# Attention by two pairs of heads in quarters of the TensorE array, beside a bilinear feed-forward network

## The chip, the cores and the metric

One core of a Trainium2 chip. The metric is the device time of one launch in microseconds (us); lower is better.

TensorE is called PE here, ScalarE ACT, VectorE DVE, GpSimd POOL; "PEld" in a profile is PE's loading of weights. "FFN" is the feed-forward network.

## The reference, cut to what matters

```python
batch, n_heads, seq, head_dim = (8, 12, 448, 64)          # q, k, v float32
n_tokens, d_model, d_ff = (3584, 768, 1536)               # w_a, w_b, w_out float64

q_n, k_n = rmsnorm(q, g_q), rmsnorm(k, g_k)               # over head_dim
scores = q_n @ k_n.T / sqrt(64)
attn = softmax(scores)
x = (attn @ v) as (8 * 448, 12 * 64)
out = ((x @ w_a) * (x @ w_b)) @ w_out
```

## The kernel before

A small planner inside the kernel (`Plan`) takes every operation with an estimated time, an engine, a priority and the tiles it needs. It plays the run through and then emits the instructions in the order it found. The order on each engine is therefore fixed when the kernel is built.

There are eight batches of twelve heads. Two batches make a block. Attention of a block has to be complete before its FFN (Strassen-like, seven products for eight) can start; the FFN of one block and the attention of the next are put between each other. At the start there is no FFN to put anywhere, and DVE has 18 weight factors to round there and in the first FFN.

Attention in the kernel before takes a pair of heads at a time, with 112 of the 448 keys as one piece:

```python
def scores(p, c, chain):                       # piece c of 4, two heads on two halves of the rows
    t = scs[p, c] = ps_s.tile([SP, 2, 512], FP32, tag="sc", name="sc")       # SP = 112
    for e in range(2):
        rows = slice(e * D, (e + 1) * D)                                     # D = 64
        nc.tensor.matmul(t[:, e, 0:S], lhsT=qkTs[p][rows, 1, c * SP:(c + 1) * SP],
                         rhs=qkTs[p][rows, 0, :], start=True, stop=True)
    # ... then ACT: E = exp(scale of the key * score)

def values(p, c, chain):                       # two heads on two halves of the columns
    for e in range(2):
        nc.tensor.matmul(os_[p][e * D:(e + 1) * D, :], lhsT=xs["v", p][:, e, c * D:(c + 1) * D],
                         rhs=ETs[p, c][:, e], start=(c == 0), stop=(c == NJ - 1))

def sums_over_keys(p, cs, chain):              # same form as values
    parts = [ETs[p, c] for c in cs] if p < WIDE else [sums[p]]     # first 12 pairs: all on PE
    for n, x in enumerate(parts):
        for e in range(2):
            nc.tensor.matmul(sus[p][e * D:(e + 1) * D, :], lhsT=ones, rhs=x[:, e], ...)
    # ... then: ACT copies the sums to a tile "rec" (3 buffers); one row per head goes by DMA
    # onto many partitions, DVE takes reciprocals there, and two DMAs bring them back into "rec"
```

A fp32 matmul is two passes of the array in the trace. Three forms of the array are in use: full (128 rows, 128 columns: FFN and transposes), rows (two heads on 64 rows each: scores), columns (two heads on 64 columns each: values and sums).

Of the kernel before, what the change touches and what calls it, by code (L numbers as in the profile page):

```python
# [25 lines left out]
class Plan:  # L26
# [11 lines left out]
    RATE, LANDING = 300.0, 2.5  # L38
# [32 lines left out]
    def run(self):  # L71
# [40 lines left out]
        while any(cands.values()):  # L112
            best = None
            for e, cs in cands.items():
                f = free.get(e, 0.0) if e else 0.0
                at = {}
                for n in cs:
                    t = buffers(n)
                    if t is not None:
                        t = t[0]  # L120
                        turn = self.TURN if ops[n][5] != modes.get(e) else 0.0
                        at[n] = max(f, ready[n], t, port if ops[n][10] else 0.0,
                                    sent[ops[n][11] - 1 - self.LANES] if ops[n][11] else 0.0) + turn
                if at:
                    t = min(at.values()) + (0.2 if e == "PE" else 0.05)
                    n = min((n for n in at if at[n] <= t), key=lambda n: (ops[n][2], n))
                    if best is None or at[n] < best[0]:
                        best = at[n], e, n
# [38 lines left out]
def kernel(  # L167
# [53 lines left out]
    ones = const.tile([SP, D], FP32, name="ones")  # L221
    gain = const.tile([P, 1], FP32, name="gain")
    expo = const.tile([SP, 2 * 2 * NJ], FP32, name="expo")
# [25 lines left out]
    ROUND, FACTOR, SQUARE, ADD_UP, TIMES = "DVE", "DVE", "ACT", "POOL", "POOL"  # L249
# [45 lines left out]
    def fast_body(ld, wk, ps_s, ps_o, ps_mm, dram):  # L295
        plan = Plan()
        op, tile_of = plan.op, plan.tile
        NORM = 4.0
        FEW = S // 8
        WARM = 4  # L300
        APART = 4
        LEAD = 12
        WIDE = 12
# [38 lines left out]
        def factors(n, key, early, after):  # L342

            last = n >= len(order)
            st = tile_of(f"st{n}", "st", 3)

            def begin():
                sts[n] = ld.tile([P, 7, KH * P], FP32, tag="st", name="st", bufs=3)
# [10 lines left out]
            for part in range(2):  # L359
# [9 lines left out]
                op("ACT", 0.45, key - 1.5, load, after, [f"{row}/{part}"], kb=768)  # L369
# [21 lines left out]
        def stream(beta, n, f=None):  # L391

            st = tile_of(f"st{beta}.{n}", "st", 3)

            def load():
                t = sts[beta, n] = ld.tile([P, 7, KH * P], FP32, tag="st", name="st", bufs=3)
# [5 lines left out]
            op("SP", 0.5, 12.0 * beta + n / 2, load, reads, [f"{st}/{x}" for x in range(7)] + ["streaming"], new=[st],  # L402
# [3 lines left out]
        xs, rs, qns, qkTs, pts, scs, ETs, sums, sus, os_, quads, hTs = ({} for _ in range(12))  # L406

        def loads(p, nm):
            b, h0 = p // HP, 2 * (p % HP)
            src = {"q": q, "k": k, "v": v}[nm]  # L410
            t = tile_of(f"{nm}{p}", nm, 2)

            def emit():
                if nm == "k":
                    x = ld.tile([SP, NJ, 2, D], FP32, tag=nm, name=nm + "_sb")
                    nc.sync.dma_start(x, src[b, h0:h0 + 2].rearrange("h (p j) d -> p j h d", j=NJ))
                else:
                    x = ld.tile([SP, 2, NJ * D], FP32, tag=nm, name=nm + "_sb")
                    nc.sync.dma_start(x, src[b, h0:h0 + 2].rearrange("h (p j) d -> p h (j d)", j=NJ))
                xs[nm, p] = x  # L420
            op("SP", 0.5 if nm != "k" else 0.9, p - (2.3 if nm == "v" else 2.5), emit, [], [t], new=[t], kb=230 if nm != "k" else 400)

        def normalize(p):
# [4 lines left out]
            def begin():  # L428
                rs[p] = wk.tile([SP, 2, 2 * NJ], FP32, tag="ms", name="ms", bufs=3)
            op(None, 0.0, key, begin, [], [f"{ms}/q", f"{ms}/k"], new=[ms])  # L430

            def sums(s, nm):
                sq = tile_of(f"sq{nm}{p}", "sq", 1)

                def square():
                    x = xs[nm, p]
                    t = xs["sq", nm, p] = wk.tile([SP, 2 * NJ, D], FP32, tag="sq", name="sq")
# [3 lines left out]
                op("ACT", 0.65, key, square, [f"{nm}{p}"], [sq], new=[sq])  # L441
                op("DVE", 0.69, key, lambda: nc.vector.tensor_reduce(rs[p][:, s], xs["sq", nm, p], AX, ALU.add), [sq], [f"{ms}/{nm}"])  # L442

            def roots(a, b, names):
                msf = lambda: rs[p][:, a:b].rearrange("p s n -> p (s n)")
                op("DVE", 0.18, key, lambda: nc.vector.tensor_scalar(msf(), msf(), 1.0 / D, 1e-6, ALU.mult, ALU.add), [], names)  # L446
                op("POOL", 1.7 if b - a == 1 else 2.95, key,
                   lambda: nc.gpsimd.tensor_tensor(msf(), msf(), expo[:, 0:2 * NJ * (b - a)], ALU.pow), [], names)  # L448

            def apply():  # L450
                qns[p] = wk.tile([SP, NJ, 2, D], FP32, tag="qn", name="qn")
# [3 lines left out]
                    rs[p][:, 0].rearrange("p (h j) -> p h j ()", j=NJ).to_broadcast([SP, 2, NJ, D]),  # L455
                    ALU.mult)
            sums(0, "q")
            if p < APART:
                roots(0, 1, [f"{ms}/q"])
            sums(1, "k")  # L460
# [5 lines left out]
            op("DVE", 0.7, key, apply, [f"{ms}/q", f"q{p}"], [qn], new=[qn], lock=True)  # L466

        def transposes(p):
            qkT = tile_of(f"qkT{p}", "qkT", 2)
            key = p - 0.5 if p < LEAD else p - 1.5  # L470
            for n, nm in ((1, "k"), (0, "q")):

                pt = f"pt{nm}{p}" if p < LEAD else f"pt{p}"
                own = n == 1 or p < LEAD
                if own:
                    tile_of(pt, *(("mm", 2) if p < LEAD else ("sc", 2)))

                def turn(n=n, nm=nm):
                    if p < LEAD:
                        t = pts[p, n] = ps_mm.tile([P, 512], FP32, tag="mm", name="pt")  # L480
                    else:
                        if n == 1:
                            pts[p] = ps_s.tile([P, 2, 512], FP32, tag="sc", name="pt")
                        t = pts[p, n] = pts[p][:, n]
                    x = xs["k", p] if n == 1 else qns[p]
                    for j in range(NJ):
                        nc.tensor.transpose(t[:, j * SP:(j + 1) * SP], x[:, j].rearrange("p h d -> p (h d)"), ident[0:SP, 0:SP])  # L487

                def take(n=n):
                    if n == 1:  # L490
                        qkTs[p] = wk.tile([P, 2, S], FP32, tag="qkT", name="qkT", bufs=2)
                        nc.scalar.copy(qkTs[p][:, 1], pts[p, 1][:, 0:S])
                    else:
                        nc.scalar.activation(qkTs[p][:, 0], pts[p, 0][:, 0:S], AF.Copy, scale=gain[:, 0:1])  # L494
                after = [] if p < LEAD else [f"half{p - 1}"]
                op("PE", 0.45, key, turn, [f"{nm}{p}" if n else f"qn{p}"] + after, [f"{pt}/{n}"], new=[pt] if own else [],
                   mode="full", chain=f"T{p}")
                op("ACT", 0.55 if n else 0.68, key, take, [f"{pt}/{n}", "gain"], [f"{qkT}/{n}"], new=[qkT] if n else [])

        def scores(p, c, chain):  # L500
            sc, E = tile_of(f"sc{p}.{c}", "sc", 2), tile_of(f"E{p}.{c}", "ET", 4)

            def product():
                t = scs[p, c] = ps_s.tile([SP, 2, 512], FP32, tag="sc", name="sc")
                for e in range(2):
                    rows = slice(e * D, (e + 1) * D)
                    nc.tensor.matmul(t[:, e, 0:S], lhsT=qkTs[p][rows, 1, c * SP:(c + 1) * SP],  # L507
                                     rhs=qkTs[p][rows, 0, :], start=True, stop=True)

            def exps():  # L510
                E = ETs[p, c] = wk.tile([SP, 2, S], FP32, tag="ET", name="ET", bufs=4)
                for e in range(2):
                    nc.scalar.activation(E[:, e], scs[p, c][:, e, 0:S], AF.Exp,  # L513
                                         scale=rs[p][:, 1, 2 * c + e:2 * c + e + 1])
            op("PE", 0.76, p, product, [f"qkT{p}/0", f"qkT{p}/1"], [sc] + ([f"scored{p}"] if c == NJ - 1 else [f"half{p}"] if c == 1 else []), new=[sc],
               mode="rows", chain=chain)
            op("ACT", 1.12, p, exps, [sc, f"ms{p}/k"], [E], new=[E])

        def values(p, c, chain):
            o = f"o{p}"  # L520
            if c == 0:
                tile_of(o, "o", 1)

            def product():
                if c == 0:
                    os_[p] = ps_o.tile([P, S], FP32, tag="o", name="o")
                for e in range(2):
                    nc.tensor.matmul(os_[p][e * D:(e + 1) * D, :], lhsT=xs["v", p][:, e, c * D:(c + 1) * D],  # L528
                                     rhs=ETs[p, c][:, e], start=(c == 0), stop=(c == NJ - 1))
            op("PE", 0.76, p, product, [f"E{p}.{c}", f"v{p}"], [o], new=[o] if c == 0 else [], mode="cols", chain=chain)  # L530

        def add_up(p, c):

            t = f"sum{p}"
            if c == 1:
                tile_of(t, "sum", 1)

            def emit():
                if c == 1:
                    sums[p] = wk.tile([P, 2, S], FP32, tag="sum", name="sum")[0:SP]  # L540
                    nc.vector.tensor_tensor(sums[p], ETs[p, 0], ETs[p, 1], ALU.add)  # L541
                else:
                    two[ADD_UP].tensor_tensor(sums[p], sums[p], ETs[p, c], ALU.add)  # L543
            if c == 1:
                op("DVE", 1.12, p, emit, [f"E{p}.0", f"E{p}.1"], [t], new=[t], lock=True)
            else:
# [510 lines left out]
```

## Time and profile before

| what | before |
|---|---|
| median of the runs beside the changed kernel | 1600.88 us |
| profiled run | 1599.5 us |
| PE, DVE, ACT, POOL busy | 99, 46, 27, 25% |
| holes of PE | nearly all before 175 us and after the last matmul |

One more view is needed for the comparison later: for whom PE's matmuls waited in the kernel before (columns: engine, line and tile that waited, who released it, us in total, times, longest).

```profile
PE sc L507 <- ACT qkT L494: 8.0, 5, 4.3
PE pt L487 <- ACT ET L513: 2.1, 1, 2.1
PE warm L872 <- POOL expo L232: 1.4, 1, 1.4
PE pq L783 <- DVE U L811: 0.6, 1, 0.6
```

That is 12 us in eight waits. This PE is fed.

### The profile page before, as it was taken

What the parts mean: (1) busy time and instruction counts of PE and PEld (TensorE: products, weight loads), DVE (VectorE), ACT (ScalarE), POOL (GpSimd) and SP (SyncE); (2) the same over time, 40 slices, a digit from 0 to 9 for tenths busy, and PEclk for the clock granted to TensorE, in tenths of its full rate; (3) what the DMA queues carried; (4) which work ended last, traced back from release to release, by engine and by line L of the source; (5) the groups of instructions that cost most, each with busy time, mean ns of one, the idle gap of its engine ahead of it and who ended that gap; (6) DMA issues with size and microseconds to landing.
All of it is one profiled execution on the core that took longest, in us unless ns stands there. A gap on an engine that the chain in (4) does not pass through costs nothing.

```text
span 1599.5 us, 14956 instructions
## 1 busy us (share of the span) xinstructions
PE 1579.5 (99%) x5482; PEld 779.8 (49%) x5482; DVE 728.5 (46%) x996; ACT 435.3 (27%) x777; POOL 398.6 (25%) x204
## 2 busy tenths in 40 slices
PE   9998999999999999999999999999999999999998
PEld 4333344554454555555444455555535555555554
DVE  6988578887575412222484622222236312222331
ACT  7875652112636300000646500000061000000000
POOL 4333642111736400110546600010052001000000
PEclk9999999999999999999999999999999999999999
DMA  7977244453333442121323433222212332222221
GB/s 230 310 244 233 66 133 144 174 212 138 94 115 94 141 141 103 69 104 65 100 83 90 134 125 104 104 72 101 75 60 95 134 128 80 93 91 72 90 94 46
DMA packets 131655, 191.19 MB, mean 120 GB/s; under 512 B 62196, under 2 KB 120308, under 8 KB 121844
## 3 DMA queue, kind: packets, MB, share of 16 engines
q1 hardware_dynamic: 103828, 137.06, 27.3%
q10 hardware_dynamic: 27744, 53.09, 9.1%
q8 instruction: 45, 0.74, 0.2%
q14 instruction: 38, 0.31, 0.1%
HBM read 154.01 MB, written 35.94 MB: 119 GB/s over the span
## 4 chain that ended last, share of the span: by engine, by line
PE 90%; DVE 4%; DMA 2%; POOL 2%; issue 1%; ACT 1%; SPq 0%; ACTq 0%; POOLq 0%; DVEq 0%
PE pq L783 47%; PE po L711 24%; PE sc L507 8%; PE o L528 7%; PE su L566 2%; PE pt L487 2%; POOL ms L448 2%; DMA rec<-inv 1%; DMA inv<-few 1%; DVE ms L442 1%; DVE st L377 0%; DVE qn L452 0%; DVE st L276 0%; DVE x L647 0%; DMA few<-rec 0%
## 5 line engine op out<-in xcount | busy, mean ns | idle before, releaser
L783 PE MATMUL pq<-x,st 128*128 128x448 f32 x2016 | 764.3, 541 | 0.6 <-DVE U L811 0.6
L783 PEld LDWEIGHTS pq<-x,st 128*128 128x128 f32 x2016 | 382.5, 191 | 369.1 <-issue 364.9
L513 ACT ACTIVATE ET<-sc,ms 112x448 f32<-112x448 f32 x384 | 215.9, 634 | 106.8 <-PE sc L507 94.1
L711 PE MATMUL po<-st,hT 128*128 128x384 f32 x744 | 244.0, 487 | 0.0
L831 POOL TENSOR_TENSOR hT<-hT,t 128x448 f32<-128x448 f32 x24 | 28.1, 1172 | 710.9 <-DVE t L829 710.9
L543 POOL TENSOR_TENSOR sum<-sum,ET 112x896 f32<-112x896 f32 x72 | 152.5, 2118 | 203.8 <-DVE sum L541 201.5
L448 POOL TENSOR_TENSOR ms<-ms,expo 112x16 f32<-112x16 f32 (+1 forms) x52 | 161.2, 3101 | 122.1 <-DVE ms L446 107.8
L711 PEld LDWEIGHTS po<-st,hT 128*128 128x128 f32 x744 | 140.8, 190 | 98.0 <-issue 2.9
L507 PE MATMUL sc<-qkT 64*112 64x448 f32 x768 | 171.2, 564 | 8.0 <-ACT qkT L494 8.0
L528 PE MATMUL o<-ET,v_sb 112*64 112x448 f32 x768 | 164.7, 550 | 0.0
L711 PE MATMUL po<-st,fin 128*128 128x384 f32 x432 | 142.4, 487 | 0.0
L805 ACT COPY hT<-pq 128x448 f32<-128x448 f32 x24 | 12.8, 532 | 421.4 <-PE pq L783 421.4
L507 PEld LDWEIGHTS sc<-qkT 64*112 64x112 f32 x768 | 61.2, 174 | 103.7 <-issue 65.1
L711 PEld LDWEIGHTS po<-st,fin 128*128 128x128 f32 x432 | 81.7, 190 | 55.2
L528 PEld LDWEIGHTS o<-ET,v_sb 112*64 112x64 f32 x768 | 50.2, 137 | 102.3 <-issue 96.7
L731 DVE TENSOR_TENSOR o_sb<-fin,po 128x384 f32<-128x384 f32 x56 | 31.0, 554 | 145.8 <-PE po L711 142.4
L442 DVE TENSOR_REDUCE ms<-sq 112x8 f32<-112x512 f32 x96 | 65.3, 680 | 35.3 <-ACT sq L440 32.9
L843 POOL TENSOR_TENSOR hT<-hT,t 128x448 f32<-128x448 f32 x48 | 57.4, 1197 | 49.1 <-DVE t L840 49.1
L452 DVE TENSOR_TENSOR qn<-q_sb,ms 112x512 f32<-112x512 f32 x48 | 47.8, 996 | 31.3 <-POOL ms L448 29.0
L808 ACT COPY t<-pq 128x448 f32<-128x448 f32 x24 | 12.8, 533 | 177.7 <-PE pq L783 177.7
L840 DVE TENSOR_TENSOR t<-U,pq 128x448 f32<-128x448 f32 x48 | 29.8, 620 | 68.8 <-PE pq L783 64.5
L836 DVE TENSOR_TENSOR hT<-U,pq 128x448 f32<-128x448 f32 x48 | 29.8, 621 | 66.2 <-PE pq L783 66.2
(70 smaller groups left out, 979.0 us busy)
## 6 DMA issues: line engine op xcount, KB each, us to landing
st<-kept SPq DMA_DIRECT2D x36, 1344.0 KB
st<-kept_o SPq DMA_DIRECT2D x28, 1152.0 KB
kept<-st ACTq DMA_DIRECT2D x12, 1344.0 KB
q_sb<-in_q_dram SPq DMA_DIRECT2D x48, 224.0 KB
k_sb<-in_k_dram SPq DMA_DIRECT2D x48, 224.0 KB
v_sb<-in_v_dram SPq DMA_DIRECT2D x48, 224.0 KB
rec<-inv SPq DMA_DIRECT2D x88, 112.0 KB
lraw<-in_moe_w_a_dram ACTq DMA_DIRECT2D x12, 768.0 KB
```

The costliest lines, as they stand in the source:

```text
L442: op("DVE", 0.69, key, lambda: nc.vector.tensor_reduce(rs[p][:, s], xs["sq", nm, p], AX, ALU.add), [sq], [f"{ms}/{nm}"])
L448: lambda: nc.gpsimd.tensor_tensor(msf(), msf(), expo[:, 0:2 * NJ * (b - a)], ALU.pow), [], names)
L452: nc.vector.tensor_tensor(qns[p].rearrange("p j h d -> p h j d"), xs["q", p].rearrange("p h (j d) -> p h j d", d=D), rs[p][:, 0].rearrange ...
L487: nc.tensor.transpose(t[:, j * SP:(j + 1) * SP], x[:, j].rearrange("p h d -> p (h d)"), ident[0:SP, 0:SP])
L507: nc.tensor.matmul(t[:, e, 0:S], lhsT=qkTs[p][rows, 1, c * SP:(c + 1) * SP], rhs=qkTs[p][rows, 0, :], start=True, stop=True)
L513: nc.scalar.activation(E[:, e], scs[p, c][:, e, 0:S], AF.Exp, scale=rs[p][:, 1, 2 * c + e:2 * c + e + 1])
L528: nc.tensor.matmul(os_[p][e * D:(e + 1) * D, :], lhsT=xs["v", p][:, e, c * D:(c + 1) * D], rhs=ETs[p, c][:, e], start=(c == 0), stop=(c == ...
L543: two[ADD_UP].tensor_tensor(sums[p], sums[p], ETs[p, c], ALU.add)
L566: nc.tensor.matmul(sus[p][e * D:(e + 1) * D, :], lhsT=ones, rhs=x[:, e], start=(first and n == 0), stop=(last and n == len(parts) - 1))
L711: nc.tensor.matmul(held["po"][:, 0:HALF], lhsT=a[0]()[:, c], rhs=sts[beta, 12 + place_of[f]][:, c], start=(c == 0), stop=(c == MH - 1))
L783: nc.tensor.matmul(banks[bank][:, 0:S], lhsT=sts[at][:, f, c * P:(c + 1) * P], rhs=quads[x][:, c], start=(start and c == 0), stop=(stop an ...
L843: lambda i=i, n=n, nm=nm: two[TIMES].tensor_tensor(C(i, n), C(i, n), held[nm], ALU.mult), [t], [hp[i]],
```

## The change

The intent: keep all four quarters of the array busy and let scores, values and sums share one form. 64 keys make a piece (7 pieces instead of 4), two pairs of heads lie on the two halves of the partitions, and each unit of work is four products of 64x64. Units fall in number, and the changes of form between scores and values vanish. Buffers had to shrink to make room: tiles for q and k from two to one each, for the reciprocals from three to one (each of double size), weight factors in work from three to two. The planner gets a penalty (`STAY`) for leaving the quarter form, and believes in a landing of DMAs of 2.0 us rather than 2.5. The core of the diff, with cuts:

```diff
-    RATE, LANDING = 300.0, 2.5
+    RATE, LANDING = 300.0, 2.0
+    STAY = 0.3
...
-        WIDE = 12
+        STS, XS = 2, 9
+        WIDE = 5
+        ADD_UP = [None, 'DVE', 'POOL', 'DVE', 'POOL', 'DVE', 'DVE']
...
-            t = tile_of(f"{nm}{p}", nm, 2)
+            t = tile_of(f"{nm}{p}", nm, 2 if nm == "v" else 1)
...
+        def scores(p, j):
             def product():
-                t = scs[p, c] = ps_s.tile([SP, 2, 512], FP32, tag="sc", name="sc")
+                t = scs[p, j] = ps_s.tile([P, 2, 512], FP32, tag="sc", name="sc")
+                for w in range(2):
+                    for e in range(2):
+                        nc.tensor.matmul(t[low_high[w], e, 0:S], lhsT=qkTs[p][low_high[e], 1, j * P + w * D:j * P + (w + 1) * D],
+                                         rhs=qkTs[p][low_high[e], 0, w * S:(w + 1) * S], start=True, stop=True)
...
+        def values(p, j):
+                for w in range(2):
+                    for e in range(2):
+                        nc.tensor.matmul(os_[p][low_high[e], w, 0:S], lhsT=xs["v", p][low_high[w], e, j * D:(j + 1) * D],
+                                         rhs=ETs[p, j][low_high[w], e], start=(j == 0), stop=(j == NT - 1))
...
+        def sums_over_keys(p, j):     # j is None from quadruple WIDE on: one product of the added keys
+                if j is None:
+                    t = ps_s.tile([P, 2, 512], FP32, tag="sc", name="su")     # a bank of the scores
...
+                for w in range(2):
+                    for e in range(2):
+                        nc.tensor.matmul(sus[p][w][low_high[e], :], lhsT=ones[low_high[w], :], rhs=x[low_high[w], e],
+                                         start=first, stop=last)
...
-            t, few = tile_of(f"rec{p}", "rec", 3), tile_of(f"few{p}", "few", 3)
+            t, few = tile_of(f"rec{p}", "rec", 1), tile_of(f"few{p}", "few", 2)
```

From the sixth quadruple on, the sums lie in one of the two tiles of PSUM that the scores use.

## The prediction

> **What bounds the kernel now.** I read the page's busy table and its 40 slices first, then busy time by stretch, the groups by line, one steady stretch of the timeline, and last the chain and timeline of the start.
>
> ```profile
> PE 1579.5 (99%) x5482; PEld 779.8 (49%) x5482; DVE 728.5 (46%) x996; ACT 435.3 (27%) x777; POOL 398.6 (25%) x204
> ...
> PE   9998999999999999999999999999999999999998
> ...
> DVE  6988578887575412222484622222236312222331
> ```
>
> TensorE (PE) is busy 99% of the span and in every slice; the others are under half. Only in the first eight slices (40 us each) is VectorE (DVE) nearly as full. So two stages have to be judged apart: a start of some 170 us, and the rest. The busy times by stretch (columns: stretch, its length, PE, weight load, DVE, ACT, POOL, clock, DMA share, GB/s):
>
> ```profile
> 120.00:160.00 40.00, 35.18 (x172) 14.33 (x170) 33.21 (x45) 22.66 (x42) 15.09 (x5) 0.96 0.73 233
> 160.00:200.00 40.00, 37.19 (x158) 15.03 (x160) 20.28 (x32) 25.50 (x48) 24.74 (x10) 0.91 0.26 66
> 200.00:240.00 40.00, 40.00 (x171) 17.03 (x168) 29.39 (x37) 23.03 (x41) 18.03 (x8) 1.00 0.45 134
> ...
> 1400.00:1600.00 200.00, 191.58 (x558) 105.85 (x556) 52.62 (x79) 5.64 (x11) 10.18 (x9) 0.99 0.23 79
> ```
>
> From 200 to 1400 us PE has no hole; its holes are in the start (about 20 us) and in the last output (8.4 us). Busy is not the same as efficient, so I look at what a steady pair of heads costs PE (columns: start, length, engine, line, operation and tiles, count):
>
> ```profile
> 402.61 1.76 PE L507 MATMUL sc<-qkT 64*112 64x448 f32 x8
> 404.30 0.97 PE L566 MATMUL su<-sum,ones 112*64 112x448 f32 x4
> 405.11 1.67 PE L528 MATMUL o<-ET,v_sb 112*64 112x448 f32 x8
> 406.71 1.76 PE L507 MATMUL sc<-qkT 64*112 64x448 f32 x8
> 408.40 1.73 PE L528 MATMUL o<-ET,v_sb 112*64 112x448 f32 x8
> 410.06 0.60 PE L487 MATMUL pt<-ident,k_sb 112*128 112x112 f32 x4
> 410.50 0.55 PE L487 MATMUL pt<-ident,qn 112*128 112x112 f32 x4
> 410.88 2.43 PE L783 MATMUL pq<-x,st 128*128 128x448 f32 x6
> 413.24 1.76 PE L507 MATMUL sc<-qkT 64*112 64x448 f32 x8
> ```
>
> Starts count here, not lengths, since ends overlap. Each fp32 matmul is two passes. A "unit" is what the array does at once: two heads' scores on two halves of its rows (64*112), or two heads' values on two halves of its columns (112*64), four passes. The single records show two passes starting 6 ns apart and the next two 0.376 us later, so a unit is 0.752 us. But two score units take 1.69 us from start to next start, not 1.50: 0.19 us is paid on entering and leaving the row form. Values entered from scores take 1.66.
>
> **What the Trainium skill says.** "TensorEngine Tiling (Array Packing)", Key Properties: "Mode switching requires drain", and tiles run independently. The trace agrees with both: 0.15 to 0.19 us extra at a change of form, none between sums and values, which share one. "TensorE: Matmul & The Clock Gate", Part 3, The mechanism: tiles of different position start about 4 ns apart. The trace shows 6 to 7 ns for two tiles; no run here shows four, and that is the disputed point. "DMA: Bandwidth & Descriptors", Anatomy of one DMA, puts about 2 us of fixed cost on a DMA; the chain here shows 2.60 us for the last hop of the reciprocal's round trip when it is quiet and 7.72 us when the start's weight loads compete.
>
> **The change part by part.** The instruction order of the built kernels gives counts without times.
>
> *Units.* Blocks of 112 keys for one pair become blocks of 64 keys for two pairs; the four products of a block fill four 64x64 quarters. Before: 192 units of scores, 192 of values, 84 of sums = 468. After: 24 quadruples x 7 blocks = 168 and 168, and sums 5x7 + 19 = 54, together 390. If a unit of four quarters also takes 0.752 us, (468-390) x 0.752 = **58.7 us less**. 36 of it is the array filled whole (112 of 128 before), 22.6 the sums, of which fewer quadruples add all keys on PE.
>
> *Changes of form.* Before has 243 on PE (95 rows to columns, 46 columns to rows, 50 into and 50 out of the full array). After has 100, since scores, values and sums share a form: 50 in, 50 out. PE's parts before: FFN passes 2016 x 0.376 = 758 and 1176 x 0.3226 = 379.4 (from runs of 474 passes in 178.2 us and 126 in 40.65); 468 x 0.752 = 352; transposes 384 x 0.098 = 37.6; warming up 6; holes 28.4. The span less these leaves 38 us for 243 changes, 0.156 each, which fits. For the changed form I choose 0.25 (at least the 0.19 of entering, perhaps more for draining four tiles; the change's own scheduler makes leaving it dearer): 25 us. **13 us less**, with 0.16 to 0.40 giving 16 to 40.
>
> *Transposes.* 336 of 128 rows for 384 of 112: at 0.098 x 128/112 = 0.112 they are 37.6 us, **no difference**.
>
> *FFN.* The same passes: 1137.4 us.
>
> *Start.* PE needs all of block zero (6 quadruples) and DVE its roundings. DVE's work up to the last combination before the first FFN, from its instruction order and the durations without contention: before, 8 weight factors x 10.6 us (three roundings at 0.96, three at 1.755, four differences at 0.555 to 0.606) plus attention, about 141 us; it stood there at 165. After, 7 factors (74), 19 reductions at about 1.1 (20), normalizations 9 x 1.15 (10), additions of keys 10 x 1.09 (11), 12 divisions and 12 combinations at 0.63 (15), small ones (5) = about 135 us. So the FFN may start near 157, not earlier by all that PE saves. PE meanwhile has quadruples 6 and 7 to do: up to the first long FFN stretch its order holds about 140 us of work. Holes in the start: before 21; after I estimate 25, as PE has less to hide behind.
>
> *Sum.* 758 + 379.4 + 390 x 0.752 (293.3) + 37.6 + 25 + warm-up 8 + start's holes 25 + end 8.4 = 1534.7. Add 5 for stalls in the first FFN (below): **1540 us**, 60 less.
>
> **The rivals.**
>
> 1. *Four quarters do not run at once.* If passes of quarters are taken in twos, a unit costs up to 1.5 us and 390 of them 290 us more: far slower. For: eight loads and eight passes per unit instead of four and four, and two quarters share rows. Against: the loads of two tiles overlap (174 ns each, 6 ns apart), the moving data per time are the same 2 x 128 partitions as in column form, and both row and column form reach their full rate. A mild form, 0.80 per unit, costs 19 us.
>
> 2. *DVE bounds the start and the first FFN.* Weight buffers go from three to two. Factor n+2 can only be rounded once factor n's products are done, and must be ready when n+1's end, 7 x 6 x 0.376 = 15.8 us later. The path: the absolute value on ACT 1.64, six DVE roundings 8.2, three differences 1.7, and about five evictions of 0.62 in between: 14.6 to 15 us. It fits by about 1 us; POOL's products beside it (1.17 each) could use that up. Ten factors at 1 us is 10 us; I count 5.
>
> 3. *The reciprocal's round trip.* The buffer for it goes from three to one and the direct reciprocals go. Three hops, 8 us quiet, up to 20 in the start, against 18 to 20 us per quadruple. If it binds there, five rounds of 3 us add 15 us; later FFN products fill the gap.
>
> 4. *ACT.* Per quadruple 14 exponentials at 0.58, squares 2 x 1.1, copies 4.4: about 15 us, against PE's 13 to 17. It is covered where FFN products can be put between, but not in the start. With q and k single-buffered, normalization (load, square, reduction, power on POOL of some 2.7 us, product) runs in about 12 us per quadruple, inside that.
>
> **Range and chances.** Optimistic: changes at 0.16, start's holes 15, no stalls: 1516. Pessimistic: unit 0.77 (+8), changes at 0.4 (+15), holes 30, stalls 5: 1568. I take this as 8 in 10. Over 2% faster means under 1568. A loss of 28 us against my sum needs two of the rivals together, or the mild form of rival 1 with another: 0.12 for the same. Slower needs rival 1 in its hard form, which the evidence on two tiles speaks against: 0.02.
>
> **What would show it.** Right: score, value and sum passes of four quarters start within some 30 ns and the next four 0.376 us later; PE still 98 to 99% busy; the groups of scores and values shrink from 171 and 165 us to about 130 each; first long FFN stretch near 157 us; the chain from there on is PE. Wrong: units of more than 0.8 us; in the first FFN waits of PE for a weight difference or of ACT for free weights in each factor (rival 2); PE waiting in the start for the copy of sums or the return of the reciprocal (rival 3), or for exponentials (rival 4); a PE share under 96%.

## The result, and the profile after

The changed kernel has a median of 1556.3 us against 1600.88 us: a ratio of 0.9722, with a 95% interval of 0.9702 to 0.9741. A ratio here is the mean time of one kernel's fast runs over that of the other's of the same rounds, so it is not quite the ratio of the medians. The result is correct.

| what | before | after |
|---|---|---|
| median, us | 1600.88 | 1556.3 |
| profiled run, us | 1599.5 | 1553.1 |
| PE busy | 99% | 98% |
| DVE, ACT, POOL busy | 46, 27, 25% | 46, 25, 20% |
| PE passes | 5482 | 6714 |
| last combination ahead of the first FFN ends at, us | 165 | 177 |
| long uninterrupted run of FFN starts at, us | 240.0 | 232.4 |

The busy table and the slices of PE and DVE after, against those in the prediction:

```profile
PE 1518.8 (98%) x6714; PEld 790.3 (51%) x6714; DVE 715.0 (46%) x932; ACT 395.7 (25%) x637; POOL 313.6 (20%) x166
...
PE   8988999999999999999999999999999999999998
...
DVE  4887869888786412222476421222245221222421
```

PE now has more holes in the first slices. The busy times by stretch say how large (columns as in the prediction):

```profile
80.00:120.00 40.00, 35.59 (x338) 22.20 (x334) 33.53 (x42) 27.76 (x44) 8.78 (x3) 1.00 1.00 276
120.00:160.00 40.00, 34.22 (x299) 15.71 (x296) 30.28 (x38) 29.62 (x50) 26.32 (x10) 1.00 0.72 197
160.00:200.00 40.00, 37.21 (x294) 15.87 (x294) 31.38 (x36) 26.96 (x47) 20.16 (x8) 1.00 0.46 107
200.00:240.00 40.00, 39.10 (x238) 18.36 (x231) 29.29 (x37) 23.40 (x36) 18.52 (x7) 1.00 0.46 103
```

DVE is not full in them either (30 of 40 us between 120 and 160 us), nor is ACT. No engine is busy throughout there; the engines wait for each other.

What a unit costs is read in the chain of work that ended last, where quarters follow quarters (columns: start, length to the next, what, passes):

```profile
456.44 0.75 PE o L530 x8
457.19 0.75 PE sc L508 x8
457.94 0.75 PE o L530 x8
458.69 0.75 PE sc L508 x8
```

Eight passes (four quarters, two each) take 0.75 us, and nothing is paid between scores and values. The single records show four passes starting 6 to 7 ns apart, and the next four 0.376 us after the first.

And for whom PE waited after:

```profile
PE sc L508 <- ACT ET L514: 8.3, 16, 1.0
PE o L530 <- ACT ET L514: 7.7, 6, 3.9
PE sc L508 <- ACT qkT L494: 6.6, 9, 1.2
PE warm L879 <- POOL ident masks.py:199: 1.4, 1, 1.4
PE sc L508 <- ACT rec L579: 1.3, 2, 1.0
```

Before, there were 8 waits; now scores and values wait for exponentials (ET) 22 times. This view counts PE's idle time up to the modelled ends of its matmuls; the stalls below are counted from starts and come out larger.

To see what became of each term of the sum, I went over the starts of all matmul passes in both profiled runs. Each pass is charged its length in an undisturbed stretch (0.376 us in the FFN's first part, 0.3226 in its second, 0.752 us per unit of attention, 0.098 and 0.109 us per transpose). Each change of form is charged what it costs where nothing else is waited for: on the mean 0.165 us before (0.15 to 0.20 by kind), 0.177 us after. Read from undisturbed starts, entering the quarter form costs 0.145 us, leaving it 0.165 us for transposes and 0.21 us for the FFN; weighted by number that is 0.17 us, under 1 us less over 100 changes. What is left over between starts is called stall.

| us | before | after | difference | predicted after |
|---|---|---|---|---|
| FFN passes | 1137.4 | 1137.4 | 0 | 1137.4 |
| units of attention, 468 and 390 | 351.9 | 293.3 | -58.6 | 293.3 |
| transposes, warming up | 42.4 | 46.2 | +3.8 | 45.6 |
| changes of form, 243 and 100 | 40.1 | 17.7 | -22.4 | 25 |
| stalls to 175 us | 17.3 | 33.9 | +16.6 | 25 |
| stalls later | 0.6 | 16.3 | +15.7 | 5 |
| ahead of the first and behind the last start | 9.8 | 8.4 | -1.4 | 8.4 |
| sum | 1599.5 | 1553.2 | -46.3 | 1539.7 |

So 81 us were saved on PE and 32 us came back as stalls. Two profiles of the same changed kernel (this one and that of a_again below, 1553.1 and 1559.3 us) differ by 6 us of stalls, all ahead of 240 us; a stall is not known better than that.

### The profile page after: what moved, and what is told of

Its sections match the earlier page's. It is cut to its first block, busy times and chain, and to the rows that moved or that the text cites.

```text
span 1553.1 us, 16949 instructions
## 1 busy us (share of the span) xinstructions
PE 1518.8 (98%) x6714; PEld 790.3 (51%) x6714; DVE 715.0 (46%) x932; ACT 395.7 (25%) x637; POOL 313.6 (20%) x166
## 4 chain that ended last, share of the span: by engine, by line
PE 88%; DMA 4%; ACT 3%; DVE 3%; issue 1%; POOL 1%; SPq 0%; ACTq 0%; DVEq 0%; POOLq 0%
PE pq L790 48%; PE po L718 24%; PE sc L508 6%; PE o L530 6%; PE pt L487 2%; PE su L566 2%; ACT ET L514 2%; DMA q_sb<-in_q_dram 1%; DMA kept_o<-st 1%; PE warm L879 1%; DMA hraw<-in_moe_w_out_dram 1%; DVE x L636 0%; DVE sum L544 0%; DMA st<-kept_o 0%; DMA rec<-inv 0%
## 5 line engine op out<-in xcount | busy, mean ns | idle before, releaser
L514 ACT ACTIVATE ET<-sc,ms 128x448 f32<-128x448 f32 x336 | 192.2, 635 | 89.8 <-PE sc L508 64.2
L530 PE MATMUL o<-ET,v_sb 64*64 64x448 f32 x1344 | 184.7, 547 | 8.2 <-ACT ET L514 7.7
L508 PE MATMUL sc<-qkT 64*64 64x448 f32 x1344 | 176.5, 546 | 16.5 <-ACT ET L514 8.3
L457 POOL TENSOR_TENSOR ms<-ms,expo 128x14 f32<-128x14 f32 x48 | 146.3, 3051 | 190.6 <-DVE ms L455 185.7
L544 POOL TENSOR_TENSOR sum<-sum,ET 128x896 f32<-128x896 f32 x38 | 80.9, 2130 | 129.8 <-ACT ET L514 74.8
L508 PEld LDWEIGHTS sc<-qkT 64*64 64x64 f32 x1344 | 58.7, 133 | 92.6 <-issue 33.7
L530 PEld LDWEIGHTS o<-ET,v_sb 64*64 64x64 f32 x1344 | 60.0, 133 | 85.6 <-ACT ET L514 40.6
L544 DVE TENSOR_TENSOR sum<-sum,ET 128x896 f32<-128x896 f32 x57 | 62.4, 1094 | 39.2 <-POOL sum L544 30.8
L451 DVE TENSOR_REDUCE ms<-sq 128x14 f32<-128x896 f32 x48 | 51.8, 1078 | 25.0 <-ACT sq L449 25.0
```

What stands on the lines that cost most here:

```text
L451: op("DVE", 1.1, key, lambda: nc.vector.tensor_reduce(rs[p][:, s], xs["sq", nm, p], AX, ALU.add), [sq], [f"{ms}/{nm}"])
L457: lambda: nc.gpsimd.tensor_tensor(msf(), msf(), expo[:, 0:2 * NT * (b - a)], ALU.pow), [], names)
L508: nc.tensor.matmul(t[low_high[w], e, 0:S], lhsT=qkTs[p][low_high[e], 1, j * P + w * D:j * P + (w + 1) * D], rhs=qkTs[p][low_high[e], 0, w ...
L514: nc.scalar.activation(E[:, e], scs[p, j][:, e, 0:S], AF.Exp, scale=rs[p][:, 1, 2 * j + e:2 * j + e + 1])
L530: nc.tensor.matmul(os_[p][low_high[e], w, 0:S], lhsT=xs["v", p][low_high[w], e, j * D:(j + 1) * D], rhs=ETs[p, j][low_high[w], e], start=( ...
L544: two[e].tensor_tensor(sums[p], sums[p] if j > 1 else ETs[p, 0], ETs[p, j], ALU.add)
```

## The experiments

Twelve kernels ran. "Changed" below is the changed kernel; its ratio to the kernel before was 0.9722 and, on the chip of the last four runs, 0.9731. One percent of the kernel before is 16 us. a_norec, a_noqk, b_twice and b_wide10 ran on another chip than the other eight; each ratio is to the kernel before on the same chip, but the changed kernel's 0.9722 for the first eight is not from their rounds.

### Scores twice, after and before: a_twice and b_twice

What is a unit worth, and how much of it does PE hide? The scores of each piece are computed twice into the same place; the result stays right.

```diff
-                for w in range(2):
+                for w in (0, 1, 0, 1):
                     for e in range(2):
                         nc.tensor.matmul(t[low_high[w], e, 0:S], ...   # scores
```

and in the kernel before `for e in (0, 1, 0, 1)`.

> The changed kernel with each unit of scores computed twice into the same bank (the result stays right): 168 more units of four quarters. If a unit costs 0.752 us and PE sets the time, 126 us more, less what falls into PE's present stalls (up to 20 us): 1662 to 1682 us. If quarters hindered each other (1.0 us and more per unit) it would be over 1724 us; if PE were not the bound, under 1620 us.

Measured: 1652.73 us, ratio 1.0319. Over the changed kernel that is 1.0319 - 0.9722 = 6.0%, 96 us, for 126 us of work: below the expected 1662, so more was hidden than I thought. The starts show the same thing. Of 508 spacings from one unit to the next without a change of form, 424 are within 5% of 0.752 us, which is also their median; so the added work is 126.3 us, and what is left as stalls is 20.0 us where the changed kernel had 50.2.

> The kernel before with each unit of scores computed twice: 192 more units in the form of halves. In the changed kernel 126 us of added units cost 96, so 30 fell into stalls. If the kernel before is held by PE nearly everywhere (17 us of stalls in all), 192 x 0.752 = 144 us more, less 5 to 10: 1736 to 1742 us. If it hid as much, 1716 us.

Measured: 1732.4 us, ratio 1.0799: 8.0%, 128 us, for 144 us of work, so 16 us were hidden, just under the range. Stalls fell from 17.9 to 4.5 us.

What follows: in both kernels a unit is worth its 0.752 us where PE sets the pace. But the changed kernel hides 30 us of new PE work, the kernel before 16. The change turned part of what it saved into waiting for others, and this is shown, not only argued, by work that costs less than it takes.

### Two changes of form more per unit: a_forms

```diff
                 t = scs[p, j] = ps_s.tile([P, 2, 512], FP32, tag="sc", name="sc")
+                nc.tensor.matmul(t[:, 0, 500:501], lhsT=ident, rhs=ident[:, 0:1], start=True, stop=True)
```

> The changed kernel with a one-column product in the full form (into an unused column of the score bank) ahead of each of the 168 units of scores: two more changes of form each, nothing else. If sharing one form is worth what the trace says (0.16 leaving and 0.19 entering, plus some 0.1 for the small product), 168 x 0.45 = 76 us more, less up to 15 us that fall into stalls: 1617 to 1632 us. If a change of form costs nothing itself, 168 x 0.1 = 17 us more at most: about 1573 us.

Measured: 1600.77 us, ratio 0.9983; 42 us over the changed kernel, under the expected 61 to 76. The timeline of PE in an undisturbed piece (columns: start, length, engine, line, operation, count):

```profile
457.36 0.98 PE L531 MATMUL o<-ET,v_sb 64*64 64x448 f32 x8
458.27 0.38 PE L506 MATMUL sc<-ident 128*128 128x1 f32 x2
458.59 0.98 PE L509 MATMUL sc<-qkT 64*64 64x448 f32 x8
459.39 0.93 PE L531 MATMUL o<-ET,v_sb 64*64 64x448 f32 x8
460.25 0.38 PE L506 MATMUL sc<-ident 128*128 128x1 f32 x2
```

Values to values takes 459.39 - 457.36 = 2.03 us where two units are 1.50. Over all places where the units on both sides are whole, the single starts give 0.47 us at the least for the two changes with the small product, where 0.45 was worked out. It was paid less often than 168 times: 125 small products stand behind values or sums and 25 behind other scores; the 18 behind work in the full form add no change of form. 150 x 0.47 is about 70 us of work, of which 42 showed: again some 28 us went into stalls. With these two changes per unit back, the changed kernel is where the kernel before was.

### Where the stalls come from, first try: a_hold

From the sixth quadruple on the sums lie in one of two score tiles until ACT can copy them into the single tile `rec`, and that tile is free only once the reciprocals of the quadruple before have come back and been used. A second tile would be the clean experiment, but does not fit: the build asked for 170.5 kB per partition for the pool of working tiles where 167.9 were left. So the sums go into another tile at once, and `rec` is opened only for the return.

```diff
             t, few = tile_of(f"rec{p}", "rec", 1), tile_of(f"few{p}", "few", 2)
+            keep_in = "sum" if p < WIDE else "sq"
+            hold = tile_of(f"hold{p}", keep_in, 1)                         # sums are copied here
...
+                sus[p] = wk.tile([P, 2, S], FP32, tag="rec", name="rec")   # opened in come_back
```

> The changed kernel, but the sums over keys leave PSUM at once, into a tile that is idle then (the one for squares, or for the first five quadruples the one for added keys), and the single reciprocal tile is opened only when the reciprocal comes back. Theory A: PE's added stalls outside the start come from the sums sitting in one of the two score banks until the single reciprocal tile is free, so that scores and exponentials take turns on the other bank. Then the stalls from 135 us on (about 24 us over the changes of form) shrink by 8 to 14 us: 1542 to 1549 us. Theory B: they come from exponentials on ACT being too slow where no FFN product is put between. Then nothing moves by more than 3 us. Theory C: normalization is the tight chain; the borrowed tile for squares delays it, and it gets slower by some 5 us.

Measured: 1579.97 us, ratio 0.9855, 21 us slower than the changed kernel; all three theories miss. Stalls rose to 75.7 us, most of the increase before 175 us (48.9 for 33.9). The chain of waits there:

```profile
131.85 0.92 ACT qkT L492
...
136.19 12.17 DMA q_sb<-in_q_dram
148.47 0.96 ACT sq L449
149.45 1.10 DVE ms L451
```

A load of q is on the chain for 12 us. But the planner had made another order for every engine, too, so the run does not tell the borrowed tile from the new order. That is a fault of the experiment; the next ones keep the order.

### What order alone does: a_slowdma and a_land25

```diff
-    RATE, LANDING = 300.0, 2.0
+    RATE, LANDING = 200.0, 3.5      # a_slowdma;  a_land25: 300.0, 2.5
```

> The changed kernel, ordered by a plan that believes in slower transfers (200 GB/s and 3.5 us to landing in place of 300 and 2.0). Only orders change. Theory D: the start's stalls (about 31 us to 172 us) come from orders planned with transfers that are too quick (the trace has 8.6 us for q and 9.8 us for a kept factor on the chain there). Then the start gains 5 to 12 us: 1544 to 1551 us. If other waits (ACT, the score banks) set the start, within 4 us of 1556, and more changes of form (112 for 100) may even cost 2 us.

Measured: 1650.39 us, ratio 1.03; 93 us slower than the changed kernel, the opposite of what I expected.

> The changed kernel with one constant of its planner taken back: 2.5 us to landing, as in the kernel before, in place of 2.0; rate and all else stay. a_slowdma (200 GB/s and 3.5 us) cost some 94 us by order alone. If only a plan far from the hardware does that, this is within 8 us of the changed kernel. If orders here are fragile in general, 10 to 40 us slower.

Measured: 1587.56 us, ratio 0.9916, 1.85% or 30 us slower than the changed kernel on the same chip: within "fragile in general". The work of PE is 1476.9 us in both, as in the changed kernel, and changes of form are 112 and 104 for 100. The rest is stalls: 143.8 and 81.9 us. For whom PE waited in a_slowdma:

```profile
PE su L566 <- ACT rec L579: 33.2, 2, 25.4
PE sc L508 <- ACT ET L514: 24.4, 42, 1.3
PE pt L487 <- DVE qn L461: 14.5, 2, 10.5
PE sc L508 <- ACT qkT L494: 11.7, 9, 3.7
```

and in a_land25:

```profile
PE su L566 <- ACT rec L579: 16.2, 3, 6.9
PE sc L508 <- ACT ET L514: 15.7, 29, 1.3
```

The largest item is new: PE wants to make the next sums, but the old ones have not been copied into `rec`. With a single reciprocal tile and a single q tile, a plan has to hit the moments when they are free, and one that is off by a guess loses 30 to 90 us. The changed kernel's constants are a lucky or a tuned place, and theory D, that slower transfers in the plan would help, fails for both plans tried.

### The reciprocals do not come back: a_norec and a_early

Their outputs are wrong, which doesn't matter for the times. All orders are those of the changed kernel, but `come_back` does nothing and the division multiplies the values by themselves, so `rec` is free as soon as its row has been sent.

```diff
             def come_back():
-                for e in range(2):
-                    nc.sync.dma_start(sus[p][low_high[e]]..., fews[1][e:e + 1, :].to_broadcast([D, 2 * S]))
+                pass
...
-                    nc.vector.tensor_tensor(t, t, sus[p][:, w], ALU.mult)
+                    nc.vector.tensor_tensor(t, t, t, ALU.mult)
```

> The changed kernel in the same order of instructions, but the reciprocals never come back to SBUF, and the division multiplies the values by themselves (wrong on purpose): the single reciprocal tile is free as soon as its row of sums has been sent out. Theory A again, now without a new order: the sums sit in a score bank, or in FFN banks at the start, until that tile is free. Then PE's stalls shrink by 10 to 20 us: 1536 to 1546 us. If the exponentials on ACT or the loads of q and k set the pace, under 4 us: over 1552 us.

Measured: 1552.49 us, ratio 0.9675 (0.9653 to 0.9698) for 0.9722 (0.9702 to 0.9741): some 7 us faster, with intervals 0.0004 apart; between the two expectations. The run also takes away the traffic of the return (48 transfers of 224 kB), so free tile and traffic are not told apart. The turns of scores and exponentials were still in its timeline, and the reason was in ACT's order: the copy of the sums still stood where the plan had put it, behind several exponentials. Here they are in the timeline of the changed kernel (PE and ACT lines, with what ended the wait in brackets):

```profile
142.76 0.98 PE L566 MATMUL su<-sum,ones 64*64 64x448 f32 x8 [0.57 <-ACT ET L514]
...
146.52 0.98 PE L508 MATMUL sc<-qkT 64*64 64x448 f32 x8 [0.53 <-ACT ET L514]
147.32 0.93 PE L530 MATMUL o<-ET,v_sb 64*64 64x448 f32 x8
147.57 1.16 ACT L514 ACTIVATE ET<-sc,ms 128x448 f32<-128x448 f32 x2 [0.27 <-PE sc L508]
148.78 0.98 PE L508 MATMUL sc<-qkT 64*64 64x448 f32 x8 [0.53 <-ACT ET L514]
149.58 0.93 PE L530 MATMUL o<-ET,v_sb 64*64 64x448 f32 x8
...
153.64 0.96 ACT L579 COPY rec<-su 128x448 f32<-128x448 f32 x2
```

The sums are made at 142.76 and copied at 153.64. In between one score tile is left: a score, its exponentials, the next score, 2.26 us per piece (146.52 to 148.78) in place of 1.50. So a_early also moves these copies in ACT's order to directly behind their product (and behind the sending of the row before), and keeps the rest.

> As a_norec (the reciprocals do not come back, wrong on purpose), and the copies of the sums out of PSUM stand in ScalarE's order directly behind their product instead of where the plan had put them; every other order is kept. a_norec left the order of the copies as planned, late, so the score bank stayed taken. Theory A: the taken bank is what makes scores and exponentials take turns. Then the stall between 130 and 175 us (11 us) falls to 3 to 5 and that between 400 and 520 us (6 us) to about 3: 8 to 12 us less than the changed kernel. Theory B (exponentials too slow): under 4 us less.

Measured: 1549.6 us against 1559.2 for the changed kernel on the same chip (a_again), ratios 0.968 and 0.9731: about 8 us faster. In the stretch of the lines above the turns are gone:

```profile
138.41 0.93 PE L517 MATMUL sc<-qkT 64*64 64x448 f32 x8
139.16 0.93 PE L539 MATMUL o<-ET,v_sb 64*64 64x448 f32 x8
139.91 0.93 PE L517 MATMUL sc<-qkT 64*64 64x448 f32 x8
140.67 0.93 PE L539 MATMUL o<-ET,v_sb 64*64 64x448 f32 x8
```

0.75 us from start to start, and over the whole run scores wait less for exponentials than the 8.3 us in 16 waits of the changed kernel:

```profile
PE sc L517 <- ACT ET L523: 2.5, 6, 0.5
```

So the mechanism of theory A is right: the taken bank makes scores and exponentials take turns. Its worth is not. Between 130 and 175 us 9.4 us of stall are left (11.3 expected to fall to 3 to 5), and between 400 and 520 us 5.2 (7 expected to fall to 3). PE now arrives earlier at the next waits, among them one of 1.8 us for the exponentials behind a load of q, and one of 1.4 us of the first FFN products for their combination on DVE. Against a_norec, which kept the turns and had gained 0.47% where a_early gains 0.51%, removing them is worth nothing that can be measured. Where the 8 us come from is open: ahead of 130 us the stalls of a_early are 18.2 us, but those of the changed kernel's two profiles are 22.5 and 27.2.

### q and k loaded once: a_noqk and a_earlynoqk

Every quadruple uses the q and k of the first. Their outputs are wrong, which doesn't matter for the times. Orders are kept.

```diff
             def emit():
+                if nm != "v" and p:
+                    xs[nm, p] = xs[nm, 0]
+                    return
```

> The changed kernel in the same order, but q and k are loaded for the first quadruple only and used for all (wrong on purpose): takes away the waits for the single q and k tiles to be free and loaded, and their traffic. Theory E: single-buffered q and k hold up the start (the chain there waits 8.6 us for one q load); the start gains 8 to 15 us: 1541 to 1548 us. Otherwise within 4 us of 1556.

Measured: 1544.77 us, ratio 0.9633 for 0.9722: 0.9%, 14 us faster. The time is within the range of theory E, and the gain lies in the start: stalls to 175 us are 23.3 us for 33.9, and the last combination ahead of the first FFN ends at 165.6 us for 176.9. How a load stops PE is to be read in the timeline of the changed kernel:

```profile
90.07 0.95 ACT L449 ACTIVATE sq<-q_sb 128x896 f32<-128x896 f32 x1 [2.95 <-DMA q_sb<-in_q_dram]
90.92 2.19 ACT L514 ACTIVATE ET<-sc,ms 128x448 f32<-128x448 f32 x4
91.59 1.12 PE L530 MATMUL o<-ET,v_sb 64*64 64x448 f32 x5 [1.94 <-ACT ET L514]
```

ACT waits 2.95 us for q to make its squares. Four exponentials (two pieces) stand behind the squares in its order; ACT idles though the scores of the first of these pieces are there, and the values wait. "TensorE: Matmul & The Clock Gate", Part 1, Architectural detail, of the Trainium skill calls ACT and DVE strict FIFO (first in, first out), PE's queue a partial window; these lines agree for ACT and show nothing of the other two. In the chain this load is

```profile
68.99 9.84 DMA kept_o<-st
81.42 8.55 DMA q_sb<-in_q_dram
```

8.55 us for q, at a DMA share of 1.00 between 80 and 120 us; ahead of it in the chain is a 9.84 us store of a rounded weight factor. That with two q tiles the load could have gone out earlier is argued; no run has them. With q and k loaded once, values wait for exponentials hardly at all:

```profile
PE sc L511 <- ACT ET L517: 7.8, 16, 0.6
PE sc L511 <- ACT qkT L497: 5.6, 9, 1.2
PE warm L882 <- POOL ident masks.py:199: 1.4, 1, 1.4
PE su L569 <- ACT ET L517: 1.1, 2, 0.6
PE sc L511 <- ACT rec L582: 1.0, 2, 0.7
PE o L533 <- ACT ET L517: 0.9, 2, 0.5
```

The item "o <- ET" falls from 7.7 to 0.9 us; "sc <- ET", the turns, stays. The run also takes away the traffic of these loads (46 of the 48 loads of 224 kB each for q and as many for k), so buffer and traffic are not told apart.

> As a_early, and q and k loaded only once as in a_noqk (wrong on purpose). If the waits are of two kinds that add up, 20 to 26 us less than the changed kernel, with stalls of about 25 us left of 50. If they are the same wait seen twice, no more than a_early or a_noqk alone (14 us).

Measured: 1541.93 us, ratio 0.963: 1.0%, some 16 us faster than the changed kernel, with 37.9 us of stalls left. 8 and 14 do not add up to 22, and a_noqk alone has 38.5 us of stalls left: mostly the same start, shortened once. The remaining stalls do not go away when the two tiles are free in the same order; an order planned for two tiles each was not run.

### Fewer sums on PE, in the kernel before: b_wide10

```diff
-        WIDE = 12
+        WIDE = 10
```

> The kernel before with ten pairs in place of twelve whose sums over keys are all made on PE, as the changed kernel has five quadruples: 6 units less on PE, four additions of keys more on DVE and POOL in the start. If PE sets the time there, 4.5 us less: 1597 us. If the start hangs on DVE or on round trips, no gain or some us more.

Measured: 1607.84 us, ratio 1.0027 (1.0018 to 1.0036), 4 us slower with 4.5 us less work for PE. Stalls rose from 17.9 to 28.9 us. There are six additions more, not four (two on DVE, four on POOL), and the planner has made a new order. So a unit taken off PE in the start brought nothing here; whether the additions or the order cost it, this run does not tell.

### The changed kernel again: a_again

> The changed kernel itself, on the same chip as the next ones, as their measure: about 0.972 of the kernel before.

Measured: 1559.2 us, ratio 0.9731 (0.9714 to 0.9747), the measure for the runs on its chip.

No correct version beat the changed kernel. The 16 us of the wrong ones are the most that freeing the tiles could bring in this order, since these runs save traffic too. It would need another tile of 3.5 kB per partition for reciprocals and one each for q and k, and the memory is full.

## Why the prediction was right or wrong, point by point

The time, 1556.3 us, lies inside the range of 1516 to 1568 us, 16 us above the sum of 1540. That it does is in part luck: the prediction has no term for the planner's order, and with the planner's landing at 2.5 us the same PE work took 1587.56 us, outside the range. By its steps:

* **Units: right.** Four quarters run at once, 0.752 us per unit, four starts 6 to 7 ns apart; 58.6 us of work saved for 58.7. Rival 1 fell in both its forms. One sign named for it was badly chosen: the groups' busy times did not shrink from 171 and 165 us to about 130 but are 176.5 (scores) and 184.7 us (values), since lengths overlap between alternating units; only starts count.
* **Changes of form: right in kind, too dear.** 0.177 us each, not 0.25: 17.7 us for the 25 in the sum. Leaving the quarter form is dearer than entering it, as was guessed (0.165 to 0.21 for 0.145 us), but far from the planner's penalty of 0.3 us more. This is a term that was 7 us too large. The count of 243 before has 51 changes into and 51 out of the full array; 50 and 50, as written, would not add up to it.
* **Transposes and FFN: right.** 36.6 for 37.6 us, and the same passes.
* **Start: the step that failed in size and in reason.** I counted DVE's work up to the last combination and let the first FFN start "near 157, not earlier by all that PE saves". The last combination ended at 177 (183 in a_again's profile), later than before (165), and the first long stretch of FFN began at 232.4 us. DVE's amount was counted well, 133.8 us busy up to then for "about 135"; but it stood idle for 43 us there, before for 31. With q and k loaded once (a_noqk) the same DVE work, 132.0 us, is done by 165.6 us. So the start is not bound by DVE's amount of work; the chain there runs through loads, squares, powers, copies and round trips. "Holes in the start: ... after I estimate 25" measured 33.9.
* **Rival 2, rounding in the first FFN with two weight buffers: did not occur.** Stalls between 240 and 400 us are 0.0; I had added 5. The fit "by about 1 us" held.
* **Rival 3, the single reciprocal tile: occurred, and not only where I put it.** "Later FFN products fill the gap" was wrong. An FFN product can fill a gap only if the order has one there, and in the stretches of scores and values above the planner had put none. Stalls after 175 us are 16.3 us, where the sum had 5. Most of them are not this tile's: 13.1 us are left in a_earlynoqk, with the tile free in the same order. a_norec and a_early make the tile, with the traffic of the return, worth about 8 us in all.
* **Rival 4, ACT and the single tiles of q and k: half right.** I wrote that normalization runs "in about 12 us per quadruple, inside that". With the loads at 8.6 us it does not: a_noqk, which also drops the traffic, is 14 us faster. The sign "PE waiting ... for exponentials" came true, 16 us in 22 waits.
* **The sum.** Work 1476.9 for 1476.3; changes 7 less; stalls 50.2 for 30; ends 8.4 for 8.4. These differences make 13.5 us, and 1539.7 + 13.5 is the profiled 1553.2. What was mis-sized is the stalls.
* **A reading.** PE was not 99% busy "in every slice": the prediction's own line has an 8 (80 to 89%) in the fourth and the last.

What stays open: how the 38 us of stalls that are left in a_earlynoqk divide; 25 lie ahead of 175 us, 13 later. Scores that wait for the copies of q and k after the transposes are 6.1 us of the waits there, and part may be ACT's pace without FFN products between; no run separates these. Nor is it known how much of a_hold's loss was order.

## What to carry to other kernels

Before counting what a freer engine gains, ask which stretches it sets the pace in: adding work there on purpose (each score twice) tells at once, since work that costs less than it takes is being hidden. When buffers are cut to pay for a better use of the array, follow the single tiles through queues that run in order: one load that is late stops the squares, the exponentials behind them and then the matmuls. And where a planner fixes the order, an experiment that changes its inputs measures the new order first; keep the order and change only the thing in question.

## What the Trainium skill lacked or had wrong

* "TensorEngine Tiling (Array Packing)", Key Properties, says that a change of tiling mode drains but gives no cost. Here it is 0.15 to 0.20 us between full, rows and columns, 0.145 entering quarters of 64x64, and 0.165 (for transposes) to 0.21 (for the FFN) leaving them.
* "TensorE: Matmul & The Clock Gate", Part 3, The mechanism, gives about 4 ns between the starts of tiles. Two halves and four quarters of fp32 passes start 6 to 7 ns apart here.
* No page that I read says how the two passes of a fp32 matmul fall when tiles are used: all tiles' first passes start together and all second ones 0.376 us later (448 columns), so four products of 64x64 with 448 columns take 0.752 us, no more than two of half the array.
* "DMA: Bandwidth & Descriptors", Anatomy of one DMA, fits about 2 us plus size over bandwidth for a DMA that GpSimd issues, and has no term for transfers beside each other. Those here are issued by SyncE and ScalarE. In the chain of the changed kernel's start a load of q (two of 224 kB) shows 8.55 us at 81 us, with a DMA share of 1.00 between 80 and 120 us, and 3.72 us at 146 us, with a share of 0.72 between 120 and 160 us.
